# Windowed attention: the exponentials that bypass ScalarE are evaluated as a fourth power, and the scheduler's rules are given per chunk

## The chip, the cores and the metric

One core of a Trainium2 chip runs the whole kernel. The metric is device time in microseconds, the median of three runs: 1099.44 us before (1097.98, 1099.44, 1100.51). A core has five engines with queues of their own: TensorE (PE; its weight loads are PEld), VectorE (DVE), ScalarE (ACT), GpSimd (POOL) and SyncE (SP, here the issuer of most DMAs). They meet through semaphores only.

## The reference

The input x is a 224 x 224 image with 96 channels in bf16. One projection gives q, k and v. The first 48 channels attend within horizontal stripes of 8 rows, the last 48 within vertical stripes of 8 columns; there are 28 stripes of each kind, and each has 8 x 224 = 1792 tokens. Both results go side by side through wo.

```python
qkv = jnp.einsum('bhwc,cd->bhwd', x, wqkv)
scale = C2 ** (-0.5)                      # C2 = 48
ah = _softmax(jnp.einsum('bqc,bkc->bqk', qh, kh) * scale, axis=-1)
oh = jnp.einsum('bqk,bkc->bqc', ah, vh).reshape(B, H, W, C2)
...                                       # the same over vertical stripes: ov
return jnp.einsum('bhwc,cd->bhwd', o, wo) # o: oh in channels 0-47, ov in 48-95
```

So every stripe needs 1792 x 1792 exponentials, 56 stripes of them; they are most of the work.

## The kernel before

The 56 stripes are worked through as 28 pairs: 14 horizontal pairs, then 14 vertical ones. A pair's two stripes ("windows") lie on partitions 0-63 and 64-127 of the q and k tiles. Queries are cut into four chunks (512, 512, 512 and 256), keys into 14 tiles of 128. One **tile** of scores is 128 keys x 512 queries x 2 windows, 128x1024 fp32 in two PSUM banks (in the last chunk a tile takes two key tiles of 256 queries). That makes 49 tiles a pair and 1372 in all. The scores are transposed (keys on partitions), already scaled to base 2 by alpha in the k evaluation (L426), and a constant column of q and k shifts them.

Each tile takes one of two ways to its exponential, which ends as a bf16 tile PT:

- **On ScalarE (kind A).** TensorE computes scores into bank pair 0-1 or 2-3 (`qk_fn`, L619, 49 rows of contraction). ScalarE takes one Exp of 128x1024 (L842), and `activation` scales by ln 2.
- **Off ScalarE (kind P or R).** Banks 6-7 serve this way (`PB0`). TensorE computes the scores into them (`s_fn`, L632); VectorE reads the low 16 bits of each fp32 score, which hold the fraction of u, into an fp16 tile qb (p1, L1123). GpSimd then evaluates a cubic: q*q (L1050), a scalar add and multiply (L1051), times q (L1052). TensorE computes the same scores once more with a few extra constant rows (L632 again), and VectorE multiplies by 128, adds the polynomial and writes a 16-bit integer whose bits are the bf16 exponential (f, L1147). An R tile has a second VectorE read (p2, L1136) and a single GpSimd square (L1049) in place of the three.

Afterwards TensorE multiplies PT by v (PV, L645) into bank 4 or 5, with the sum of the exponentials in a 49th column. VectorE evicts the result (L1105), TensorE applies wo (L504, L540), and VectorE divides by the sum (L511 and L519 for horizontal stripes, kept in SBUF as Ph_sb; L547 and L552 for vertical ones, which add Ph_sb and go out by DMA). The fills that prepare the next pair (transposes, k, q, v: L404, L421, L468) are put between.

The order on every engine is fixed when the program is built. `Sched` keeps planned times with a cost for each operation (D_ACT, D_MM, D_P1 = 1.135, D_SQ = 1.9, D_AF = 1.03, D_ML = 2.08 us); `step_pe`, `step_dve` and `step_pool` pick the next operation of the engine that is free first in the plan. On the chip each engine runs its list in that order and waits on semaphores. `HOW` has one tuple of eleven parameters for each pair: `step_pe` reads when to change between scores and PV (B1, B2, B3), how many POOL operations may wait before another off tile is opened (PBACK), when to keep a bank (KEEP) and how many off tiles may be ahead (PAHEAD); an index into `KINDS` says which tiles of each chunk go off ScalarE (always the last ones of a chunk); one parameter (`how()[10]`, 0 for every pair) would let a ScalarE tile use banks 6-7 as a third set (L940 and on), and another spreads out the next pair's fills.

`KINDS` and `HOW` give 198 off tiles: 189 P and 9 R. ScalarE takes the other 1174. There are NPT = 24 buffers PT and NQB = 5 buffers qb. A PT buffer is taken for an off tile with its first scores and given back at its PV.

## Time and profile before

| | |
|---|---|
| median of three runs | 1099.44 us |
| profiled execution: span from first to last instruction | 1093.9 us (its time outside the span isn't listed) |
| mean granted TensorE clock | 1.000 |
| ScalarE exponentials | 1174, the first starts at 8.5 us, the last at 1086.3 |
| off tiles | 198 |
| GpSimd, four groups of off-tile work | 402.0 + 358.1 + 197.8 + 17.0 us |
| VectorE, p1 and f | 241.9 + 242.0 us |

How to read it. "Busy" is time in which at least one instruction of an engine runs; instructions of one engine overlap at their ends, so the mean duration of an exponential (1088 ns) is more than its share of the busy time (1078.3 us / 1174). In a group's row stand line, engine, operation, what it writes and reads with the shapes, the count, then busy us and mean ns, then the engine's idle time just before these instructions and who ended it. PE is busy in the records whenever a matmul is under way, whose end is modelled. Bank numbers and buffer numbers are left out of names: `ps` is PSUM, `PT` any of the exponential tiles.

### The profile page before, as it was taken

To read this page: it belongs to the slowest core of one execution; us is meant where nothing else is said; L and a number is where in the kernel's file an instruction comes from. 1 tells how busy PE (TensorE), PEld (TensorE's weight loads), DVE (VectorE), ACT (ScalarE), POOL (GpSimd) and SP (SyncE) were. 2 spreads that over 40 slices of the span, in tenths; PEclk is the share of its full clock that TensorE was granted. 3 is DMA by queue.
4 is the path that set the end of the run, shared out by engine and by line. 5 is a ranking of instruction groups with operands and counts; after the bars stand their busy time and mean duration, and the time that the engine had idled before them with its cause. 6 is when DMAs were issued, how large, how long until landed. Compare 5 with 4: busy or idle time off the path is not lost.

```text
span 1093.9 us, 35292 instructions
## 1 busy us (share of the span) xinstructions
PE 1048.7 (96%) x14788; PEld 421.1 (38%) x14788; DVE 922.5 (84%) x1694; ACT 1082.6 (99%) x1185; POOL 974.7 (89%) x613
## 2 busy tenths in 40 slices
PE   8999999999999999999999999999999999999997
PEld 3344443444434443443433333333333433343333
DVE  7788888888888887888898888889889888989885
ACT  8999999999999999999999999999999999999997
POOL 7999899979999979979989999977997899987993
PEclk9999999999999999999999999999999999999999
DMA  5231232033023123211001111202111211211111
GB/s 97 37 52 21 34 53 45 10 52 52 15 40 52 20 35 53 39 30 39 27 2 39 27 41 43 46 17 53 39 30 38 47 42 44 45 26 30 33 21 33
DMA packets 183799, 40.91 MB, mean 37 GB/s; under 512 B 180408, under 2 KB 180952, under 8 KB 183640
## 3 DMA queue, kind: packets, MB, share of 16 engines
q1 hardware_dynamic: 182520, 38.17, 18.3%
q8 instruction: 116, 1.90, 0.7%
q10 hardware_dynamic: 1120, 0.49, 0.2%
q14 instruction: 43, 0.35, 0.1%
HBM read 19.36 MB, written 19.27 MB: 35 GB/s over the span
## 4 chain that ended last, share of the span: by engine, by line
PE 44%; ACT 39%; issue 9%; POOL 4%; DVE 4%; DMA 0%; ACTq 0%; POOLq 0%; DVEq 0%
ACT PT L842 39%; PE ps L619 17%; PE ps L645 16%; PE ps L632 4%; PE ps L421 2%; POOL PT L1052 2%; PE ps L468 2%; POOL PT L1050 1%; PE ps L404 1%; DVE PT L1147 1%; DVE qb L1123 1%; PE ps L504 1%; POOL PT L1051 1%; DVE out_all L552 1%; PE ps L450 1%
## 5 line engine op out<-in xcount | busy, mean ns | idle before, releaser
L842 ACT ACTIVATE PT<-ps 128x1024 bf16<-128x1024 f32 x1174 | 1078.3, 1088 | 1.5 <-PE ps L619 1.2
L619 PE MATMUL ps<-QT_sb,KT_sb 49*64 49x512 bf16 (+1 forms) x5480 | 481.8, 366 | 36.9 <-ACT PT L842 23.9
L645 PE MATMUL ps<-PT,V_sb 128*49 128x512 bf16 (+1 forms) x3136 | 440.7, 360 | 0.1
L1052 POOL TENSOR_TENSOR PT<-PT,qb 128x1024 f16<-128x1024 f16 x189 | 402.0, 2127 | 15.7
L1050 POOL TENSOR_TENSOR PT<-qb 128x1024 f16<-128x1024 f16 x189 | 358.1, 1895 | 64.3 <-DVE qb L1123 33.1
L1147 DVE SCALAR_TENSOR_TENSOR PT<-ps,PT 128x1024 uint16<-128x1024 f32 x198 | 242.0, 1222 | 57.7 <-PE ps L632 41.9
L619 PEld LDWEIGHTS ps<-QT_sb,KT_sb 49*64 49x64 bf16 x5480 | 139.2, 103 | 380.4 <-ACT PT L842 362.9
L1123 DVE TENSOR_SCALAR qb<-ps 128x1024 f16<-128x1024 int16 x198 | 241.9, 1222 | 41.4 <-PE ps L632 39.1
L1051 POOL TENSOR_SCALAR PT<-PT 128x1024 f16<-128x1024 f16 x189 | 197.8, 1046 | 16.6
L645 PEld LDWEIGHTS ps<-PT,V_sb 128*49 128x49 bf16 x3136 | 128.0, 103 | 169.6 <-issue 136.0
L632 PE MATMUL ps<-QT_sb,KT_sb 50*64 50x512 bf16 (+2 forms) x1584 | 154.7, 380 | 1.4 <-DVE PT L1147 0.6
L552 DVE SCALAR_TENSOR_TENSOR out_all<-ps,rc,Ph_sb 128x96 bf16<-128x96 f32 x392 | 96.5, 310 | 2.8
L1105 DVE CAST OT_sb<-ps 113x512 bf16<-113x512 f32 x112 | 69.6, 621 | 18.2 <-PE ps L645 16.7
L437 DVE CAST QT_sb<-ps 128x512 bf16<-128x512 f32 (+1 forms) x111 | 67.2, 617 | 15.7 <-PE ps L421 15.2
L426 DVE TENSOR_SCALAR_CACHE_REDUCE KT_sb<-ps 128x512 bf16<-128x512 f32 x108 | 65.0, 618 | 8.2 <-PE ps L421 7.9
L519 DVE TENSOR_TENSOR Ph_sb<-ps,rc 128x480 bf16<-128x480 f32 (+1 forms) x84 | 52.3, 622 | 2.5
L475 DVE CAST V_sb<-ps 128x480 bf16<-128x480 f32 (+1 forms) x84 | 51.6, 620 | 2.7 <-PE ps L468 2.2
L632 PEld LDWEIGHTS ps<-QT_sb,KT_sb 50*64 50x64 bf16 (+2 forms) x1584 | 45.6, 105 | 13.5 <-DVE PT L1147 4.6
L468 PEld LDWEIGHTS ps<-w_sb,xT_sb 96*64 96x64 bf16 x1568 | 33.4, 112 | 17.9 <-issue 12.6
L421 PE MATMUL ps<-xT_sb,wq_sb 97*64 97x512 bf16 x224 | 40.0, 367 | 0.0
L468 PE MATMUL ps<-w_sb,xT_sb 96*64 96x48 bf16 x1568 | 39.7, 191 | 0.0
L421 PE MATMUL ps<-xT_sb,w_sb 97*64 97x512 bf16 x224 | 39.3, 366 | 0.1
(64 smaller groups left out, 359.6 us busy)
## 6 DMA issues: line engine op xcount, KB each, us to landing
xT_sb<-xt_dram SPq DMA_DIRECT2D x28, 336.0 KB, 4.1
out_dram<-out_all SPq DMA_DIRECT2D x386, 24.0 KB, 1.9
out_all<-in_x_dram SPq DMA_DIRECT2D x52, 168.0 KB, 2.7
xt_dram<-xT_sb SPq DMA_DIRECT2D x26, 336.0 KB, 5.6
xt_dram<-xT_sb SPq DMA_DIRECT2D x4, 168.0 KB, 4.2
Ph_sb<-in_x_dram SPq DMA_DIRECT2D x2, 168.0 KB, 3.5
Ph_sb<-in_x_dram ACTq DMA_DIRECT2D x2, 168.0 KB, 3.8
out_dram<-out_all ACTq DMA_DIRECT2D x6, 24.0 KB, 1.9
```

Source lines behind the costliest of these rows:

```text
L421: ins = e.matmul(bk[64 * w:64 * w + 64, 0:qs], lhsT=lw, rhs=xT_sb[b][:, w, q0:q0 + qs], start=True, stop=True)
L468: ins = e.matmul(bk[64 * h:64 * h + 64, j * C2:(j + 1) * C2], lhsT=xT_sb[b][0:C, w, t0:t0 + 64], rhs=w_sb[0:C, wblk(P, "v"), 0:C2], start= ...
L552: return e.scalar_tensor_tensor(out_sb[b][:, w, kt, :], bk3[:, s, 0:C], rc[ri][:, s:s + 1], Ph_sb[:, kt, j, :], ALU.mult, ALU.add)
L619: ins = e.matmul(bank(SETS[s] + w)[64 * kh:64 * kh + 64, i * t["qs"]:(i + 1) * t["qs"]], lhsT=KT_sb[b][64 * w:64 * w + CA, kt * 128 + 64 * ...
L632: ins = e.matmul(bank(PB0 + w)[64 * kh:64 * kh + 64, 0:512], lhsT=KT_sb[b][64 * w:64 * w + nr, kt * 128 + 64 * kh:kt * 128 + 64 * kh + 64] ...
L645: ins = e.matmul(bank(pb)[64 * w:64 * w + CA, 0:t["qs"]], lhsT=V_sb[b][:, w, kt, :], rhs=PT[slot][:, ca:ca + t["qs"]], start=st and i == 0 ...
L842: S.commit("act", 0.0, D_ACT, None, lambda e, s=s, slot=slot: e.activation(PT[slot][:], ps[:, 512 * SETS[s]:512 * SETS[s] + 1024], ACTF.Ex ...
L1050: sq = lambda e: e.tensor_tensor(y, q, q, ALU.mult)
L1051: af = lambda e: e.tensor_scalar(y, y, PB, 128.0 * PA, ALU.add, ALU.mult)
L1052: ml = lambda e: e.tensor_tensor(y, y, q, ALU.mult)
L1123: S.commit("dve", t, D_P1, D_P1 + SEMD + (0.12 if tl["kind"] == "R" else 0.0), lambda e: e.tensor_scalar(qb[tl["qb"]][:], low16(), m, a, A ...
L1147: S.commit("dve", t, D_P1, D_P1 + SEMD, lambda e: e.scalar_tensor_tensor(PT[tl["slot"]][:].bitcast(U16), ps[:, PB0 * 512:(PB0 + 2) * 512], ...
```

## The change

Four things change.

1. **The evaluation off ScalarE.** alpha is 128 times larger, and ScalarE's scale is divided by 128. With the new constants in the extra column (21 of k, 32 of q, times alpha) the fp32 score is 128 (u + 140): the upper 16 bits, read as bf16, are 128 times the whole part, and the lower 16 bits, read as unsigned, are the fraction. p1 writes q = QS (fraction + QH) in **fp32**; GpSimd squares q in place in fp32 and then squares it into an fp16 tile, a fourth power in place of the cubic; f adds a constant and that tile to the upper halves. Both score passes contract over 50 rows. The R kind is gone, with p2.
2. **Buffers.** qb is fp32, NQB stays 5; NPT goes from 24 to 21.
3. **Setup.** One extra column in place of four: fewer memsets of constants.
4. **The plan.** `OFF` gives the number of off tiles for each pair and chunk; `TAIL` the spread of the fills for each pair; `RULES` gives the nine parameters for each pair and chunk. `how()[7]` (was `[10]`) lets ScalarE's scores use banks 6-7 in the chunks where it is 1 or 2.

```diff
-PA, PB, PK, PC = 0.07791904306483502, -6.713656137731462, 0.9677202424844896, 0.435546875
-RA, RB, RS, RK = 0.0284523, 8.8088709, 0.06682159, 0.08613579
-HS = RS * 128.0 ** 0.5 * 2.0 ** -16
+QK, QH, QC0 = 0.00302015814, 3.83652076, 0.346271089
+QS = (128.0 * QK) ** 0.25
+SOFF = 140.0
-KINDS = ["PP PP PP ", "PPP PP PP ", "PPP PPP PP ", "PP PP P ", ...
-NPT = 24
+NPT = 21
-D_P1, D_SQ, D_AF, D_ML = 1.135, 1.9, 1.03, 2.08
+D_P1, D_SQ = 1.135, 1.9
 HOW = [
-    (4, 7, 9, 2, 1, 5, 2, 1, 1, 0.06, 0), (4, 7, 2, 2, 1, 6, 2, 1, 0, 0.06, 0), ...
+    ("113", 10, "269216002 489216002 393229100 358228000"),
+    ("313", 4, "358228003 258228000 395127102 395127102"),
...
+    ("422", 11, "493428000 491428100 366315100 266435100"),
 ]
+OFF = [[int(d) for d in k] + [0] for k, _, _ in HOW]
+TAIL = [t for _, t, _ in HOW]
+RULES = [[[int(d, 16) for d in r[:8]] + [(0.0, 0.03, 0.06, 0.1)[int(r[8])]] for r in rs.split()] for _, _, rs in HOW]
...
-    alpha = float(C2) ** -0.5 / LN2
+    alpha = 128.0 * float(C2) ** -0.5 / LN2
...
-        qb = [sb(f"qb{i}", [128, 1024], FP16) for i in range(NQB)]
+        qb = [sb(f"qb{i}", [128, 1024], FP32) for i in range(NQB)]
...
-        KC = [4.8125, 31.25, -45.5, 2.09375, 1.6796875]
-        QC = [0.0, 21.0, 1.0, 1.0, -1.4921875]
+        KC = [4.8125 / 128.0, 21.0]
+        QC = [0.0, 32.0]
...
-                off = KINDS[HOW[P][7]][c]
-                na = len(groups) - len(off)
+                off = OFF[P][c]
+                na = len(groups) - off
...
-                PT[slot][:], ps[:, 512 * SETS[s]:512 * SETS[s] + 1024], ACTF.Exp, scale=LN2),
+                PT[slot][:], ps[:, 512 * SETS[s]:512 * SETS[s] + 1024], ACTF.Exp, scale=LN2 / 128.0),
...
         def how():
-            return HOW[act_seq[min(ia[0], len(act_seq) - 1)]["P"]]
+            tl = act_seq[min(ia[0], len(act_seq) - 1)]
+            return RULES[tl["P"]][tl["c"]]
...
-                    if qstart > t + 0.1 and how()[10] and not p_wants() and PB0 in frb and PB0 + 1 in frb and \
-                            not (how()[10] == 1 and s2_q and s2_q[0]["ready"] <= t + 1.6):
+                    if qstart > t + 0.1 and how()[7] and not p_wants() and PB0 in frb and PB0 + 1 in frb and \
+                            not (how()[7] == 1 and s2_q and s2_q[0]["ready"] <= t + 1.6):
                         qset, qstart = 2, max(t, kr)
...
-            if tl["kind"] == "R":
-                yk = pt_keys(tl["slot"])
-                return [("pool", D_SQ, lambda e: e.tensor_tensor(y, y, y, ALU.mult), yk + ["pser"], yk)]
-            sq = lambda e: e.tensor_tensor(y, q, q, ALU.mult)
-            af = lambda e: e.tensor_scalar(y, y, PB, 128.0 * PA, ALU.add, ALU.mult)
-            ml = lambda e: e.tensor_tensor(y, y, q, ALU.mult)
             qk, yk = [("q", i), "pser"], pt_keys(tl["slot"])
-            return [("pool", D_SQ, sq, qk, yk), ("pool", D_AF, af, yk, yk), ("pool", D_ML, ml, qk + yk, yk)]
+            return [("pool", D_SQ, lambda e: e.tensor_tensor(q, q, q, ALU.mult), qk, [("q", i)]),
+                    ("pool", D_SQ, lambda e: e.tensor_tensor(y, q, q, ALU.mult), qk, yk)]
...
-                m, a = (HS * 2.0 ** -16, HS * RB) if tl["kind"] == "R" else (2.0 ** -16, 0.5 + PK)
-                S.commit("dve", t, D_P1, D_P1 + SEMD + (0.12 if tl["kind"] == "R" else 0.0), lambda e: e.tensor_scalar(
-                    qb[tl["qb"]][:], low16(), m, a, ALU.mult, ALU.add),
+                S.commit("dve", t, D_P1, D_P1 + SEMD, lambda e: e.tensor_scalar(
+                    qb[tl["qb"]][:], half(U16, 0), QS * 2.0 ** -16, QS * QH, ALU.mult, ALU.add),
...
-                    PT[tl["slot"]][:].bitcast(U16), ps[:, PB0 * 512:(PB0 + 2) * 512], 128.0,
-                    PT[tl["slot"]][:].bitcast(FP16), ALU.mult, ALU.add),
+                    PT[tl["slot"]][:].bitcast(U16), half(BF16, 1), 128.0 * (126.0 - SOFF + QC0),
+                    PT[tl["slot"]][:].bitcast(FP16), ALU.add, ALU.add),
```

`half(dt, i)` is a view of banks 6-7 as 16-bit elements, every second one. For a P tile before, qb was given back after the third GpSimd operation; now it is after the second square.

## The prediction

> **What bounds it now.** I read the page's busy shares first, then the costliest groups, then ScalarE's own waits, and last what waits for GpSimd's results. The page:

> ```profile
> span 1093.9 us, 35292 instructions
> PE 1048.7 (96%) x14788; PEld 421.1 (38%) x14788; DVE 922.5 (84%) x1694; ACT 1082.6 (99%) x1185; POOL 974.7 (89%) x613
> PEclk9999999999999999999999999999999999999999
> ```

> ScalarE is busy for 99% of the span; the granted clock is full throughout. PE's 96% is no second bound: matmul ends are modelled, and the group of score matmuls below says what its loads wait for. The groups:

> ```profile
> L842 ACT ACTIVATE PT<-ps 128x1024 bf16<-128x1024 f32 x1174 | 1078.3, 1088 | 1.5 <-PE ps L619 1.2
> L1052 POOL TENSOR_TENSOR PT<-PT,qb 128x1024 f16<-128x1024 f16 x189 | 402.0, 2127 | 15.7
> L1050 POOL TENSOR_TENSOR PT<-qb 128x1024 f16<-128x1024 f16 x189 | 358.1, 1895 | 64.3 <-DVE qb L1123 33.1
> L1147 DVE SCALAR_TENSOR_TENSOR PT<-ps,PT 128x1024 uint16<-128x1024 f32 x198 | 242.0, 1222 | 57.7 <-PE ps L632 41.9
> L619 PEld LDWEIGHTS ps<-QT_sb,KT_sb 49*64 49x64 bf16 x5480 | 139.2, 103 | 380.4 <-ACT PT L842 362.9
> L1123 DVE TENSOR_SCALAR qb<-ps 128x1024 f16<-128x1024 int16 x198 | 241.9, 1222 | 41.4 <-PE ps L632 39.1
> L1051 POOL TENSOR_SCALAR PT<-PT 128x1024 f16<-128x1024 f16 x189 | 197.8, 1046 | 16.6
> ```

> The first row is nearly the span: 1174 exponentials in 1078.3 us, idle 1.5 us before them. One lasts 1088 ns but they overlap; 1078.3 / 1174 = 0.9185 us is what one costs. In the trace's starts, 1000 of the 1173 steps from one exponential to the next are at most 925 ns (mean 908.5); the other 173 are later, by 10.0 us in all over 921 ns. So the stage has a floor of some 0.91 us a tile and about 10 us of lateness. The PEld row shows PE's cover: score loads wait 362.9 us for ScalarE to release a bank pair, not the reverse. The span is then 8.5 us of lead, 1174 exponentials, 6.5 us of tail (last exponential's end at 1087.3 to 1093.9).

> **Counting the change.** There are 28 x 49 = 1372 tiles. Before, 198 (189 P, 9 R) go round ScalarE. The digits of the new table add up to 66 + 68 + 78 = 212 for the first three chunks, none in the fourth. ScalarE keeps 1372 - 212 = 1160: 14 fewer.

> ScalarE: 14 x 0.9185 = 12.9 us off the path, since this engine has no idle to absorb it. Both kernels use the same shape and bank layout; only the scale constant changes, by the 128 that alpha now carries.

> GpSimd, per P tile: before 1.895 + 1.046 + 2.127 = 5.07 us; after, two squares. Neither an fp32 input nor an fp32 output of this size is in the trace. Two inputs of the same tile in fp16 take 1.895 (L1050; the in-place L1049 is 1.894). From below I allow the one-input L1051, 1.046; from above twice 1.895, 3.79, should four-byte elements need twice the passes. The row nearest in kind is this one:

> ```profile
> L288 POOL MEMSET xT_sb<- 1x1792 f32 x1 | 1.6, 1587 | 0.4 <-DVE wq_sb L262 0.4
> L292 POOL COPY wq_sb<-wst 96x96 bf16<-96x96 bf16 x4 | 1.1, 264 | 0.2
> L301 POOL COPY w_sb<-wst 96x192 bf16<-96x192 bf16 x1 | 0.3, 341 | 1.2 <-DMA wst<-in_wqkv_dram 1.2
> ```

> Columns: count, then busy us and mean ns. The two copies differ by 96 elements and 77 ns: 0.80 ns an element over a fixed 187 ns. The fp32 memset writes at most 1587 / 1792 = 0.89 ns an element, so four bytes cost about what two do. L1050 over the same fixed part is (1895 - 187) / 1024 = 1.67 ns, two such passes. I take 1.895 for each square. GpSimd is then 212 x 3.79 = 803 us where it was 402.0 + 358.1 + 197.8 + 17.0 = 975: 171 us lighter, off the path. Per tile the chain from first evaluation to last shrinks by 1.28 us.

> [...]

> VectorE: 14 more tiles with two evaluations each. Back to back, their starts are 1.141 us apart, so 28 x 1.141 = 31.9 us more; 9 second reads of the R kind go, 10.3 us less. Its idle after the lead is 161 us, and 161 - 21.7 - 12.9 leaves some 126. The fp32 qb write and the bf16 strided read aren't in the trace: L1136, a strided int16 read beside an SBUF operand, takes 1218; the VectorE memset of 256 four-byte words takes 272, about one a nanosecond. I take 1.222 as now; doubled writes (2.4) would fill the 126 us, and I see no row for that.

> TensorE: an off tile's scores are computed twice, so 14 x 4 more matmuls; in the timeline around 500 us such a set follows another after 0.24 us: 3.4 us. With the 12.9 us shorter span that is 16 us out of at most 363 us of waiting: hidden, unless the order makes it late (a rival). Contraction over 50 rows for 50, 52 or 53 costs nothing either way: all three sit in one row, L632.

> Setup: six memsets of 60 ns go from VectorE and nine of 103 ns from GpSimd. They lie ahead of the landing of x and wqkv (L301 waits 1.2 us for it): 0, at best 0.4. No DMA is added, removed or moved past another in SP's or ScalarE's queue, except as whole pairs come sooner.

> Buffers: 24 to 21 exponential tiles. An off tile holds one during its GpSimd chain, which drops 1.28 us; ScalarE's waits name no PV (L645) now, so I take 0, and put what may go wrong into the give-back rival. A help: the first square no longer writes such a tile. L1050 waited 22.4 us, four times, for PV to clear one; GpSimd has that time to spare now.

> Rules: parameters per chunk in place of per pair, and in 36 of 112 chunks ScalarE's scores may use banks 6 and 7 as a third set, which none could before. Below, all 10 us of late steps could go; above, lateness may grow as the two uses collide. Without a row that favours either I take lateness per tile as now, contained in 0.9185.

> **Sum.** 1093.9 - 12.9 = 1081.0 us of span. The time of the profiled execution outside its span isn't listed; the median of the three runs is 1099.44, 5.5 us above this span, and I carry that: 1086.5, called **1086**.

> **Rivals.**
> - **Fewer late steps.** GpSimd had 89% and is now at 74%, and a third bank pair exists. If the 10 us go entirely: 1076.5; half: 1081.5. Against: PE's shown waits name ScalarE's release, not lack of scores, and more off tiles crowd VectorE. 14%.
> - **Late squares.** The order on each engine is fixed ahead with 1.9 us for a square. If it takes 2.127, as L1052, the last evaluation L1147 has its input 0.46 us late. This is the present cover:

> ```profile
> L1147 DVE SCALAR_TENSOR_TENSOR PT<-ps,PT x198: 1194/1225/1227, 21.0 to 1076.3; 128x1024 uint16<-128x1024 f32 x198
> ...
>   POOL PT L1051: 1.2, 2
>   POOL PT L1050: 0.6, 1
>   POOL PT L1052: 0.2, 1
>   POOL PT L1049: 0.2, 1
> ```

>   These are the waits of L1147 by releaser, us and times: for GpSimd 2.2 us in all, so results are ready first. In the starts, the median time from a finished L1052 to the next L1147 is 1.49 us, a tenth are under 0.44. Subtracting 0.46 from each leaves 0.025 us a tile, 212 x 0.025 = 5 us, if all of it reaches ScalarE: 1092. [...] Against: the element rates above. 12%.
> - **Given back.** Extra scores and the third bank pair stand ahead of L619 in PE's fixed order, and 21 tiles are fewer. Break-even is 1078.3 / 1160 = 0.9296 us a tile: lateness up from 10.0 to 22.9 us. Doubled lateness gives 1096. For it: each off tile holds banks 6 and 7 twice; against: the 363 us. 11%.
> - **GpSimd becomes the bound**, which ends slower. Place: the two squares. GpSimd's work spans all but some 33 us of the span (first at 14, last end at 1075), so 424 squares reach the old time from (1099.4 - 5.5 - 33) / 424 = 2.50 us each. At 3.79 it is 1607 + 33 + 5.5 = 1645. For it: four-byte elements; against: the memset. 5%.

> **Chances and range.** The forecast, 1082 to 1091, has 58%. A measurement can tell about 0.2% from no change, so faster means under 1097.2. Faster: 58 + 14 + 8 of the late squares + 5 of the give-back = 85%; within: 2 + 3 = 5%; slower: 2 + 3 + 5 = 10%. The range goes from 1077 (most lateness gone) to 1097 (lateness doubled); the bound and the outer late squares are left out.

> **What would show it.** Right: 1160 rows of the exponential at about 0.919 us each, idle before them under 3 us; squares at 1.9 us in two groups of 212; GpSimd near 74%, VectorE near 87%. Wrong: squares over 2.1 us with L1147 waiting for GpSimd; more than 20 us over 921 ns between exponentials; ScalarE waiting for PV, which would be the 21 tiles; VectorE's first evaluation over 1.3 us, which would be the fp32 write.

## The result, and the profile after

| | before | after |
|---|---|---|
| median of four runs | 1098.71 us (1097.75 to 1100.51) | 1085.45 us (1085.13 to 1087.20) |
| span of the profiled execution | 1093.9 us | 1083.4 us (of a run of 1085.23) |
| first exponential starts, last one ends | 8.5, 1087.3 us | 9.4, 1076.3 us |
| steps between exponentials over 925 ns; what they add over 921 ns | 173; 10.0 us | 182; 10.9 us |

The ratio is 0.988 (95% interval 0.9865 to 0.9896): faster by 1.2%. The prediction said 1086. The medians in this document are over all executions of a kernel; the ratios leave out the one slow execution that there was, 1148.64 us of late_squares.

The page of the changed kernel opens so:

```profile
span 1083.4 us, 35256 instructions
PE 1048.3 (97%) x14838; PEld 427.5 (39%) x14838; DVE 944.6 (87%) x1707; ACT 1071.1 (99%) x1171; POOL 804.7 (74%) x452
PEclk9999999999999999999999999999999999999999
```

ScalarE is as full as it was, GpSimd went from 89% to 74%, VectorE from 84% to 87%. The groups that answer to those of before (line numbers are 10 to 20 higher; the columns are the same: count, busy us, mean ns, idle before and its releaser):

```profile
L861 ACT ACTIVATE PT<-ps 128x1024 bf16<-128x1024 f32 x1160 | 1066.5, 1081 | 1.3 <-PE ps L638 1.1
L1068 POOL TENSOR_TENSOR qb<-qb 128x1024 f32<-128x1024 f32 x212 | 401.2, 1892 | 232.8 <-DVE qb L1134 173.6
L1069 POOL TENSOR_TENSOR PT<-qb 128x1024 f16<-128x1024 f32 x212 | 401.2, 1893 | 25.7 <-POOL qb L1068 4.2
L1144 DVE SCALAR_TENSOR_TENSOR PT<-ps,PT 128x1024 uint16<-128x1024 bf16 x212 | 259.0, 1222 | 41.5 <-PE ps L651 23.6
L1134 DVE TENSOR_SCALAR qb<-ps 128x1024 f32<-128x1024 uint16 x212 | 259.0, 1221 | 31.9 <-PE ps L651 28.4
L638 PEld LDWEIGHTS ps<-QT_sb,KT_sb 49*64 49x64 bf16 x5424 | 137.5, 103 | 361.7 <-ACT PT L861 338.3
```

The first row has it: 14 exponentials fewer, 1078.3 - 1066.5 = 11.8 us less, and still only 1.3 us of idle before them. Both squares, fp32 in and fp32 or fp16 out, take what the fp16 square took (1892 and 1893 ns against 1895). GpSimd now waits 173.6 us for VectorE's first read, where 33.1 us stood before: it has stopped being short.

### The profile page after: what moved, and what is told of

Read it like the earlier page. It is cut to its first block, busy times and chain, and to the rows that moved or that the text cites. A ratio compares the mean times of both kernels' runs of the same rounds, so it can differ in the third digit from the quotient of the medians.

```text
span 1083.4 us, 35256 instructions
## 1 busy us (share of the span) xinstructions
PE 1048.3 (97%) x14838; PEld 427.5 (39%) x14838; DVE 944.6 (87%) x1707; ACT 1071.1 (99%) x1171; POOL 804.7 (74%) x452
## 4 chain that ended last, share of the span: by engine, by line
PE 52%; ACT 36%; issue 8%; DVE 3%; POOL 0%; DMA 0%; ACTq 0%; DVEq 0%
ACT PT L861 36%; PE ps L638 20%; PE ps L664 19%; PE ps L651 4%; PE ps L440 3%; PE ps L423 2%; PE ps L487 2%; PE ps L523 1%; DVE out_all L571 1%; DVE qb L1134 1%; PE ps L559 1%; DVE PT L1144 1%; PE ps L469 1%; POOL PT L1069 0%; DVE OT_sb L1117 0%
## 5 line engine op out<-in xcount | busy, mean ns | idle before, releaser
L861 ACT ACTIVATE PT<-ps 128x1024 bf16<-128x1024 f32 x1160 | 1066.5, 1081 | 1.3 <-PE ps L638 1.1
L1068 POOL TENSOR_TENSOR qb<-qb 128x1024 f32<-128x1024 f32 x212 | 401.2, 1892 | 232.8 <-DVE qb L1134 173.6
L638 PE MATMUL ps<-QT_sb,KT_sb 49*64 49x512 bf16 (+1 forms) x5424 | 475.8, 365 | 26.3 <-ACT PT L861 14.0
L664 PE MATMUL ps<-PT,V_sb 128*49 128x512 bf16 (+1 forms) x3136 | 453.5, 361 | 0.0
L1069 POOL TENSOR_TENSOR PT<-qb 128x1024 f16<-128x1024 f32 x212 | 401.2, 1893 | 25.7 <-POOL qb L1068 4.2
L1144 DVE SCALAR_TENSOR_TENSOR PT<-ps,PT 128x1024 uint16<-128x1024 bf16 x212 | 259.0, 1222 | 41.5 <-PE ps L651 23.6
L1134 DVE TENSOR_SCALAR qb<-ps 128x1024 f32<-128x1024 uint16 x212 | 259.0, 1221 | 31.9 <-PE ps L651 28.4
L638 PEld LDWEIGHTS ps<-QT_sb,KT_sb 49*64 49x64 bf16 x5424 | 137.5, 103 | 361.7 <-ACT PT L861 338.3
L651 PE MATMUL ps<-QT_sb,KT_sb 50*64 50x512 bf16 x1696 | 166.7, 381 | 0.9 <-DVE PT L1144 0.6
L456 DVE CAST QT_sb<-ps 128x512 bf16<-128x512 f32 (+1 forms) x111 | 68.0, 618 | 11.8 <-PE ps L440 11.2
L651 PEld LDWEIGHTS ps<-QT_sb,KT_sb 50*64 50x64 bf16 x1696 | 49.3, 105 | 16.7 <-DVE qb L1134 4.3
L487 PEld LDWEIGHTS ps<-w_sb,xT_sb 96*64 96x64 bf16 x1568 | 35.2, 112 | 13.3 <-issue 7.5
L429 DVE COPY xT_sb<-ps 97x896 bf16<-97x896 bf16 x52 | 32.3, 621 | 4.9 <-PE ps L423 4.5
```

Source lines behind the costliest of these rows:

```text
L487: ins = e.matmul(bk[64 * h:64 * h + 64, j * C2:(j + 1) * C2], lhsT=xT_sb[b][0:C, w, t0:t0 + 64], rhs=w_sb[0:C, wblk(P, "v"), 0:C2], start= ...
L638: ins = e.matmul(bank(SETS[s] + w)[64 * kh:64 * kh + 64, i * t["qs"]:(i + 1) * t["qs"]], lhsT=KT_sb[b][64 * w:64 * w + CA, kt * 128 + 64 * ...
L651: ins = e.matmul(bank(PB0 + w)[64 * kh:64 * kh + 64, 0:512], lhsT=KT_sb[b][64 * w:64 * w + nr, kt * 128 + 64 * kh:kt * 128 + 64 * kh + 64] ...
L664: ins = e.matmul(bank(pb)[64 * w:64 * w + CA, 0:t["qs"]], lhsT=V_sb[b][:, w, kt, :], rhs=PT[slot][:, ca:ca + t["qs"]], start=st and i == 0 ...
L861: S.commit("act", 0.0, D_ACT, None, lambda e, s=s, slot=slot: e.activation(PT[slot][:], ps[:, 512 * SETS[s]:512 * SETS[s] + 1024], ACTF.Ex ...
L1068: return [("pool", D_SQ, lambda e: e.tensor_tensor(q, q, q, ALU.mult), qk, [("q", i)]), ("pool", D_SQ, lambda e: e.tensor_tensor(y, q, q, ...
```

## The experiments

The theory: the time is ScalarE's count of exponentials times 0.92 us, and the new evaluation matters only because it lets GpSimd carry 212 tiles. The rivals: that the lighter evaluation, the rules per chunk, the third bank set or the buffers gain by themselves.

One thing must be said of the method. The order on the engines is built by a planner, and a kernel with another count or evaluation needs rules of its own. Where an experiment says "rules chosen anew", the nine parameters of each of the 112 chunks were chosen by one forward search over the planner, of the same kind and size for all such kernels. `new_eval_212` is the reference for these: the changed kernel with rules from that search.

All times are medians; the ratio is to the kernel before on the same chip. Chips differ between sets of runs, and the kernel before measured 1098.6 to 1099.1 us on them.

| kernel | evaluation | off tiles | us | ratio (95% interval) |
|---|---|---|---|---|
| old_eval_198 | cubic | 198 | 1101.33 | 1.0020 (1.0009 to 1.0031) |
| new_eval_198 | fourth power | 198 | 1101.90 | 1.0028 (1.0016 to 1.0039) |
| new_eval_212 | fourth power | 212 | 1086.83 | 0.9905 (0.9880 to 0.9930) |
| old_eval_212 | cubic | 212 | 1178.93 | 1.0749 (1.0706 to 1.0791) |

**new_eval_198.** The edit in the changed kernel (KINDS as in the kernel before; all off tiles by the fourth power):

```diff
-OFF = [[int(d) for d in k] + [0] for k, _, _ in HOW]
+OFF = [[len(k) for k in KINDS[h[7]]] for h in HOW0]
```

> The changed kernel's evaluation and buffers, but the kernel before's counts of off tiles (198), with rules per chunk chosen anew for these counts, third bank set allowed. Count theory: ScalarE keeps 1174 exponentials at 0.92 us, so 14 x 0.92 = 12.9 us above the changed kernel: 1098, within 3 us. Rival, that the lighter GpSimd chain or the rules per chunk removed late steps by themselves: 1092 or less although the count is the old one.

Measured 1101.90. **old_eval_198**, the kernel before with `how()` reading a rule per chunk:

```diff
-            return HOW[act_seq[min(ia[0], len(act_seq) - 1)]["P"]]
+            tl = act_seq[min(ia[0], len(act_seq) - 1)]
+            return RULES[tl["P"]][tl["c"]]
```

> The kernel before, its cubic on GpSimd and its 198 off tiles, with nothing but rules per chunk in place of rules per pair, chosen in the same way as in new_eval_198. Count theory: the same time as new_eval_198 within 3 us, some 1098, as ScalarE has 1174 exponentials in both. Rival, that per-chunk rules carry the gain: 1090 or less here; that the evaluation carries it at equal count: this one slower than new_eval_198 by 5 us or more.

Measured 1101.33. **new_eval_212**, the changed kernel with RULES from the common search:

> The changed kernel with its 212 off tiles, but its rules per chunk replaced by ones chosen in the way of the two other kernels of this set, so that the three differ in count and evaluation alone. Count theory: 10 to 14 us below new_eval_198 and old_eval_198, and within 5 us of the changed kernel's 1085.5. Rival, that the changed kernel's own rules carry it: no more than 5 us below the two others.

Measured 1086.83. ScalarE's rows of new_eval_198, old_eval_198 and new_eval_212, in this order:

```profile
L874 ACT ACTIVATE PT<-ps 128x1024 bf16<-128x1024 f32 x1174 | 1081.4, 1077 | 5.3 <-PE ps L651 4.4 <-PE ps L664 0.4
L874 ACT ACTIVATE PT<-ps 128x1024 bf16<-128x1024 f32 x1174 | 1081.5, 1077 | 4.4 <-PE ps L651 2.6 <-PE ps L664 0.7
L892 ACT ACTIVATE PT<-ps 128x1024 bf16<-128x1024 f32 x1160 | 1069.8, 1069 | 2.0 <-PE ps L669 1.1
```

The two evaluations at 198 tiles differ by 0.6 us, within their intervals, although GpSimd is busy for 973.4 us in the cubic's kernel and 752.2 in the other. Making GpSimd lighter is worth nothing by itself, and neither are rules per chunk: both kernels are 2 to 3 us slower than the kernel before with its own rules, with 16 us of late steps where that has 10, and new_eval_198 lies 1 us outside what was expected. The 14 tiles between new_eval_198 and new_eval_212 are worth 15.1 us, a little more than the 10 to 14 expected: 11.6 us are ScalarE's busy time in these exponentials (1081.4 to 1069.8), 3.3 its idle time before them (5.3 to 2.0).

**old_eval_212** completes the square (`off = "P" * OFF[P][c]` with the changed kernel's counts in the kernel before):

> The kernel before's cubic and its 24 buffers, but the changed kernel's 212 off tiles (all of the P kind), rules per chunk chosen anew in the same way as in the first set. It completes a square of evaluation by count. Theory: the count makes the time only while GpSimd can carry it; here GpSimd needs 212 x 5.07 = 1075 us, and with the 33 us at both ends 1108 of span: 1110 or more, higher still if lateness adds up, with VectorE's last evaluation waiting for GpSimd. Rival, that the count alone is the gain and the evaluation is neutral: 1087, as new_eval_212.

Measured 1178.93. Its groups for ScalarE and GpSimd's longest operation:

```profile
L875 ACT ACTIVATE PT<-ps 128x1024 bf16<-128x1024 f32 x1160 | 1075.4, 1067 | 75.6 <-PE ps L652 63.0 <-POOL PT L1086 9.3 <-issue 1.8
L1086 POOL TENSOR_TENSOR PT<-PT,qb 128x1024 f16<-128x1024 f16 x212 | 450.5, 2125 | 17.7
```

The same 1160 exponentials, but ScalarE sits idle for 75.6 us, 63.0 of it until scores are there. The cubic can't carry these counts: GpSimd's 1072.6 us of work and the 33 us at both ends are already more than the changed kernel's whole span, and the measured time is 69 us above the 1110 of the bare sum. VectorE's last evaluation waits for GpSimd for only 2.9 us here, so that sign of the expectation missed; it waits 54.0 us for the second scores. The plan knows how long the cubic takes and may hold these scores back, which isn't shown, and how the extra 69 us arise isn't either. So the count is the gain, and the evaluation is what pays for the count.

**no_third_212**: `_r[7] = 0` in every rule, rules chosen anew.

> new_eval_212 with ScalarE's scores never in banks 6 and 7, rules chosen anew in the same way. Theory (the third set is worth nothing, lateness per tile stays): 1086.8 within 4 us. Rival, that the third set carries part of the gain: 1092 or more.

Measured 1088.67, ratio 0.9915 (0.9885 to 0.9944), which overlaps new_eval_212's. The third bank set has no effect that these runs can tell; they lie between 1085.5 and 1091.9, so some 3 us would not show.

**old_198_21pt**: old_eval_198 with `NPT = 21`, rules chosen anew.

> old_eval_198 with 21 exponential buffers in place of 24, rules chosen anew in the same way: the buffer part of the change by itself. Theory (no wait on a buffer decides): within 4 us of old_eval_198's 1101.3. Rival, that the three buffers are cover that the longer cubic chain needs: 1108 or more, with ScalarE or GpSimd waiting for PV.

Measured 1100.03, ratio 1.0013 (0.9998 to 1.0028). At the old count and with the cubic the three buffers cost nothing; in its waits ScalarE waits for PV 0.2 us in all. They weren't given back to the changed kernel.

**pair_rules_212**: the changed kernel's evaluation and counts under the kernel before's rules.

```diff
+RULES = [[list(h[:6]) + [h[8], h[10], h[9]]] * 4 for h in HOW0]
```

> The changed kernel with its 212 off tiles and its evaluation, but the kernel before's rules, one set for each pair, as they stood; nothing chosen anew. Count theory in its bare form (ScalarE takes 1160 x 0.919 whatever the rules): 1086. Rival, that an order belongs to its evaluation and counts: late steps grow by tens of us and the time is over 1110.

Measured 1206.40, ratio 1.0982 (1.0964 to 1.1000): the bare count theory is false. The same work in another order costs 121 us (the plan also puts in 35 more warm-up matmuls, see the last section, 9.6 us of TensorE's time). No kernel with one rule for each pair chosen anew for 212 tiles was run, so whether the finer rules are needed for this count is open. ScalarE's wait row in that kernel (engine and line, whom it waited for, us, times, longest):

```profile
ACT PT L873 <- PE ps L650: 109.5, 75, 10.0
```

**new_eval_224**: 3, 3 and 2 off tiles in the first three chunks of every pair, rules chosen anew, without the third bank set.

> The new evaluation with 3, 3, 2 off tiles in the first three chunks of every pair, 224 in all, rules chosen anew, no third set. If the count were all, 12 x 0.92 = 11 us below new_eval_212: 1076. Theory: the gain ends where VectorE's two reads and TensorE's second scores no longer fit between the exponentials; VectorE had 132 us idle in new_eval_212 and loses 12 x 2 x 1.141 + 11 = 38 of it, GpSimd is at 78%: no engine is full, but late steps grow; I expect 1085 to 1105 with more than 14 us of lateness.

Measured 1112.02, ratio 1.0142 (1.0108 to 1.0176). In the profiled execution (1119.37 us, the slowest of the four) ScalarE's work fell to 1061.3 us for 1148 exponentials, but late steps rose to 47.0 us and idle before exponentials to 33.3. No engine is full: VectorE 87%, GpSimd 76%. I had expected 1085 to 1105 and missed. Which part of the order fails first isn't settled, nor whether a better search would find rules for 224.

**The squares made slower.** Three kernels put an fp32 memset of a spare buffer ahead of each of the 424 squares, which the plan isn't told:

```diff
+            def sq(e, dst):
+                nslow[0] += 1
+                e.memset(slow[nslow[0] % 3][:], 0.0)
+                return e.tensor_tensor(dst, q, q, ALU.mult)
```

**little_late** (160 elements):

> The changed kernel with a memset of 160 fp32 elements ahead of each square: some 0.23 us, which makes a square cost 2.125, the two-tile row that the prediction's late-squares rival used. The prediction priced this at 5 us by looking at each tile alone: 1090.5. If lateness adds up along GpSimd's runs of back-to-back tiles (the first-in first-out sum over the changed kernel's own trace gives 42 us as an upper bound, 188 where late_squares measured 55): some 12 us, 1098.

Measured 1094.98, ratio 0.9963 (0.9942 to 0.9984). **late_squares** (304 elements):

> The changed kernel with a memset of 304 fp32 elements ahead of each of the 424 squares, which the fixed order does not allow for: by the row of the fp32 memset some 0.35 us, so a pair of squares is 0.7 us late and GpSimd is busy for 424 x 2.24 = 950 us, still no bound. By the prediction's cover (median 1.49 us from GpSimd's result to its reader in the kernel before) at most 14 us: 1086 to 1100. If off tiles had no slack at all, 212 x 0.7 = 148 us more; if GpSimd is wholly off the path, 1085.5.

Measured 1140.44, ratio 1.0349 (1.0290 to 1.0408): 55 us above the changed kernel by medians, 52 by the ratios, where at most 14 were expected. The memset group has a mean of 351 ns, so the dose is what was meant, and GpSimd is only 82% busy. The memsets slow no other operation: the squares take 1893 ns, VectorE's two evaluations 1221 and 1223. Who held back the last evaluation, in the changed kernel and then in late_squares (releaser, us, times):

```profile
L1144 DVE SCALAR_TENSOR_TENSOR PT<-ps,PT x212: 1185/1225/1226, 22.3 to 1068.1; 128x1024 uint16<-128x1024 bf16 x106
...
  POOL qb L1068: 0.9, 2
...
  POOL PT L1069: 0.3, 1
```

```profile
L1151 DVE SCALAR_TENSOR_TENSOR PT<-ps,PT x212: 1193/1225/1226, 21.5 to 1120.0; 128x1024 uint16<-128x1024 bf16 x106
...
  POOL PT L1074: 42.5, 57
  PE ps L653: 21.1, 36
```

VectorE waits 42.5 us for GpSimd, against 1.2 us in the changed kernel; in little_late it is 11.0, in later_squares below 107.5. The timeline shows one such case, in the rows of four engines (start, length, what, idle before):

```profile
311.07 1.89 POOL L1074 TENSOR_TENSOR PT<-qb 128x1024 f16<-128x1024 f32 x1
...
313.10 1.23 DVE L1151 SCALAR_TENSOR_TENSOR PT<-ps,PT 128x1024 uint16<-128x1024 bf16 x1 [1.69 <-PE ps L640]
...
314.38 0.41 PE L442 MATMUL ps<-xT_sb,w_sb 97*64 97x512 bf16 x2 [0.98 <-DVE PT L1151]
...
315.18 1.02 ACT L863 ACTIVATE PT<-ps 128x1024 bf16<-128x1024 f32 x1 [0.87 <-PE ps L640]
```

GpSimd's second square ends at 312.96, VectorE starts 0.14 us later and had been idle for 1.69 us (the view names PE, which had long been done); TensorE's next fill waits for VectorE, and the scores for ScalarE stand behind that fill in its queue: ScalarE is idle for 0.87 us. GpSimd never waits here and nothing is full; one late result goes through three in-order queues.

**late_known**: late_squares with D_SQ = 2.25 in the plan and rules chosen anew.

> late_squares with the same memsets, so the same GpSimd work of 950 us, but the plan is told 2.25 us for a square and the rules are chosen anew for it, no third set. If the 55 us of late_squares come from lateness that the fixed order didn't allow for: back to within 10 us of new_eval_212, 1085 to 1097. If GpSimd's extra work itself is what costs: 1130 or more as in late_squares.

Measured 1106.17, ratio 1.0084 (1.0051 to 1.0118). Telling the plan brings back 34 of the 55 us by medians (29 of 52 by the ratios): those were lateness that the order didn't allow for, and VectorE's last evaluation waits for GpSimd for only 0.9 us now. The other 21 us stay, so my expectation missed: longer squares cost something even when planned (late steps of 26.3 us against 10.9, and 11.1 us from the last exponential to the end against 7.1). What sets that remainder isn't settled.

**later_squares** (780 elements):

> The changed kernel with a memset of 780 fp32 elements ahead of each square, some 0.75 us: a square costs 2.64, over the 2.50 at which the prediction's slower rival has GpSimd decide. By that rival's formula 424 x 2.64 + 33 us of ends = 1152 of span, 1154. If the order on the other engines adds to it, as in late_squares: 1200 or more, with GpSimd busy for under 95%.

Measured 1323.92, ratio 1.2050 (1.1979 to 1.2121), GpSimd busy for 83%. The formula for a full GpSimd lies 170 us under what happens.

No kernel tried beats the changed one.

## Why the prediction was right, and where it wasn't

- **ScalarE's step** (14 x 0.9185 = 12.9 us): the busy time fell by 11.8. One exponential costs 1066.5 / 1160 = 0.9194 us, as late steps added 0.9 us; "lateness per tile as now" held.
- **The span** was to be 1081.0 and is 1083.4: 0.9 us from the lateness, 0.9 from a later first exponential, 0.6 from a longer tail.
- **The time outside the span** (5.5 us carried) is the term that was mis-sized: it is 1.8 us here (1085.23 - 1083.4), and in later runs of the kernel before too (1098.56 with a span of 1096.8). With 1.8 us around it the span of 1093.9 makes some 1095.7, below all four measured times, so it will have come from a faster execution, and a step against it with a constant up to the median mixed two executions. The span was 2.4 us too short and the time around it 3.7 too long; that they nearly cancel, and the sum of 1086.5 lies within 1.1 us of the median, is in part luck. By medians the change is 13.3 us, by the two spans 10.5.
- **GpSimd** (two squares of 1.895; 803 us): 1.892 and 1.893 us, 802 in all, with both inputs the same fp32 tile.
- **VectorE** (1.222 for both reads; 126 us idle after the lead): 1.221 and 1.222, some 128 us between the first exponential and the last. The fp32 write took no longer than the fp16 one: 1.221 us against 1.222.
- **TensorE** (16 us out of the 363 us of waiting): its score loads now wait 338.3 us for ScalarE, 25 less.
- **Buffers, third set, lighter GpSimd at 0**: old_198_21pt, no_third_212 and new_eval_198 agree within some 3 us, the buffers at the old count alone. The setup's 0 wasn't tried by itself; the first exponential starts at 8.5 to 10.2 us in these profiles, whatever the kernel.
- **The late-squares rival** didn't come to pass, but its price was wrong, and by the largest factor here. The failed step is "subtracting 0.46 from each leaves 0.025 us a tile". It took every tile alone: 5 us for 2.13 us squares, and for the 2.24 of late_squares, by the same cover, at most 14. Measured: 9.5 us (little_late) and 52 to 55 us (late_squares). The outer late squares that the range left out are shown by no run: the squares took 1.892 and 1.893 us, and memsets had to make them late. GpSimd serves off tiles in runs: in the changed kernel's trace only 43 of the pauses between its 424 squares are over 1 us, so some five tiles go by from one to the next, and within a run each tile starts late by all the lateness before it. Pushing the changed kernel's own GpSimd operations back first in, first out, without letting anything else move, gives some 40 and 180 us of missing input where tile by tile gives some 5 and 14. The measured costs lie between; that the arrivals move too in a run is a reason argued, not shown.
- **The GpSimd-bound rival** priced 2.50 us as the break-even. In the changed kernel's fixed order the break-even lies between 2.13 us (1094.98) and 2.24 (1140.44), and at both GpSimd is far from full (81% and 82%): its lateness decides, not its sum.

## What to carry to other kernels

When one engine is full and work is moved off it, count what is left on that engine: here an evaluation that made the helper lighter paid nothing until the count changed, and then paid about the count (13 to 15 us for 14 exponentials of 0.92). Price a helper that may be late by its runs of back-to-back work, first in, first out, not item by item; a helper at 74% cost some 5% here when it was 0.35 us an operation slower than a fixed order allowed for. A schedule built for one set of durations and counts is part of the kernel: the same work under the old rules cost 121 us. And take a span and the time around it from the same execution.

## What the runs showed of the hardware that was not expected

In late_squares TensorE also ran slower where the order was late. Windows around the case above (us; busy time of PE, PEld, DVE, ACT and POOL with counts; then granted clock, DMA share, GB/s):

```profile
298.00:315.00 17.00, 16.02 (x230) 6.38 (x222) 13.56 (x19) 16.30 (x18) 15.13 (x14) 1.00 0.40 68
315.00:332.00 17.00, 17.00 (x176) 6.45 (x176) 9.58 (x19) 11.16 (x12) 7.89 (x9) 0.50 0.11 16
332.00:349.00 17.00, 17.00 (x262) 7.40 (x256) 14.15 (x22) 17.00 (x19) 11.12 (x11) 0.99 0.30 54
```

Right after the stall at 314 us the granted clock is 0.50 for 17 us; ScalarE gets 12 exponentials in place of the 18 and 19 of its neighbours, and then all is as before. PE reads 17.00 busy in the bad window although it runs fewer matmuls there (176 against 230 and 262): each takes longer (97 ns of busy time a matmul against 70 and 65). Over these kernels the mean clock falls as ScalarE's idle time before exponentials grows: 0.999 with 2.0 us (new_eval_212), 0.991 with 9.8 (little_late), 0.983 with 33.3 (new_eval_224), 0.974 with 41.8 (late_squares), 0.955 with 75.6 (old_eval_212), 0.929 with 113.0 (pair_rules_212), 0.874 with 200.4 (later_squares); no_third_212, at 1.000 with 7.4, is off that line. In late_squares the stretches at 0.5 last 61 us and hold 26 of its 62 us of late steps; in later_squares 336 us hold 143 of 243. Both directions fit that: a pause lowers the clock, and the low clock makes the next scores late. This may be part of why late_squares cost more than the tile-by-tile price, but no run here held the clock up by itself, so it is argued and not shown. The planner itself puts in warm-up matmuls on a zeroed tile (`warm`, L1059) where its plan leaves TensorE little to do: 10 in the changed kernel, 45 in pair_rules_212, 122 in old_eval_212. late_squares has the changed kernel's 10, since its plan knows of no lateness.

GpSimd read and wrote fp32 at the pace of fp16 in a square of one tile: 1892 ns for 128x1024 in the changed kernel against 1895 in the kernel before.
